# Prologue laid out anew: block 0 mixed half by VectorE and half by GpSimd, weight conversion and the third softmax moved into the first pairs

## Chip, core and metric

The kernel runs on one core of a Trainium2 chip. The metric is the device time of one execution in microseconds; before the change it is 2334.73 us (median of 3 runs, 2332.31 to 2334.87). The engines are named as in the profile: PE (TensorE, with its weight loads PEld), DVE (VectorE), ACT (ScalarE), POOL (GpSimd) and SP (SyncE, which issues the DMAs here).

## What is computed

The input `x` is (8, 4096, 192) in float32, `weight_gen` (8, 4096, 8, 7). A softmax over the seven taps of each token and head gives weights with which the token's row and the six rows before it are mixed, head by head (24 columns each). The result, 32768 rows of 192, goes through a feed-forward layer with 2048 hidden columns and a cosine:

```python
w = np.exp(weight_gen - max);  w = w / (sum(w) + 1e-9)      # over the 7 taps
x = einsum('bshk,bskhg->bshg', w, x_unfolded)               # causal, 7 rows
h = x @ w_in            # (32768, 192) @ (192, 2048)
g = h * np.cos(h)
return (g @ w_out).astype(np.float32)                       # (2048, 192)
```

`w_in` and `w_out` arrive as float64.

## The kernel before, in words

Each of the 128 partitions owns 256 consecutive rows. They are worked in 64 blocks of 4 rows (512 tokens of all partitions together). For each block the kernel mixes the rows (`attention`, L229), transposes the result on PE into x^T and splits it in a high part (fp32r) and a low part (`split`, L280). The hidden columns are worked in 8 pairs of 128-column chunks, so the main loop (L538) runs over 512 pairs, `i` = 0 to 511, and some turns more to drain.

One pair goes through these steps: PE computes h (`ffn_in_first` L313 and `ffn_in_second` L328, products of high and low parts); ACT writes the number of whole turns as an integer (`act_turns`, L349); DVE subtracts it from h (`dve_fraction`, L353); ACT takes the sine (`act_cos`, L357); DVE multiplies into g (`dve_g`, L360); ACT writes g's high part (`act_hi`, L367) and DVE its low part in bf16 (`dve_lo`, L371). Only then is the pair's PSUM tile free; there are three of these (`ps_h`). Six pairs later `ffn_out` (L377) multiplies g by `w_out`. `evacuate` (L409) lets ACT copy the sums out and POOL add them up.

All engines work through their instructions strictly in the order in which the program writes them, and the end of the kernel pins that order. In turn `i` of the loop the steps are written as: turns of pair i-1, high part of pair i-2, the third softmax's or a later one's Exp if it is due, the conversion of weights booked for this turn, fraction and sine of pair i-1, low part of pair i-2, g of pair i-1, then PE's work for pair i, the evacuation, the next weight load, one step of a softmax, and two to four steps of the background generator.

- **Mixing.** `attention(b, eng, ra, rb)` is written as 13 steps: a product for each of seven taps (L239) and six additions (L256), on the engine it is given. For blocks 1 to 63 this is POOL, step by step from the background generator `attentions` (L457), which also loads the rows two blocks ahead and waits for the softmax of its block.
- **Softmax.** `softmax` (L177) works on a batch of rows: a DMA of the taps, maximum (DVE, L190), subtraction (L192), Exp (ACT, L195), sum (L200), reciprocal (L206), product (L208). The first batch covers block 0, the second blocks 1 and 2, the third blocks 3 to 6; later ones four blocks each. Exp and the sine are different tables of ACT.
- **Weights.** `two_parts` (L105) turns float64 words into a float32 high part that PE can use and a low part: ACT takes the absolute value of the upper words (L116), DVE does four steps (L118, L121, L126, L130), ACT copies the high part (L132; for `w_out` also a bf16 copy, L134), POOL subtracts for the low part (L136). Its scratch tile `t1` shares four buffers with the `turn` tiles; `size` and `bits` are its two halves. The raw words land in buffers of the `ghi` tiles (`words`, L101). `w_in_a(c0, c1)` brings the first 128 rows of `w_in` for a range of columns in the layout that PE needs, `w_in_b(j)` a middle part of 512 columns, that is, for four pairs, and `w_out_2(q)` two chunks of `w_out`.
- **Booking.** The list `late` (L478) books conversions: an entry of period p is loaded two turns ahead and converted in turn p+1 (`converts`, popped with i-1).
- **Prologue** (L492 to L532). Loads: first taps, `w_in_b(0)`, `w_in_a(0, 256)`, block 0's rows, second taps, `w_in_a(256, 512)`, `w_in_b(1)`, block 1's rows, third taps, and two periods of `late`. Block 0 is mixed by POOL (row 3) and DVE (rows 0 to 2), the third softmax gets as far as its Exp, and ahead of the loop the chunks `a1` and `b1` are converted.
- **No-ops of SP.** `traded` (L266) has SP take part in the hand-over of a PSUM tile, so a no-op stands in SP's queue between the two halves of a pair, behind all DMAs issued before it.

Of the kernel before, what the change touches and what calls it, by code (L numbers as in the profile page):

```python
# [13 lines left out]
I32 = mybir.dt.int32  # L14
U16 = mybir.dt.uint16
BF16 = mybir.dt.bfloat16
AF = mybir.ActivationFunctionType
# [3 lines left out]
P = 128  # L21
# [20 lines left out]
def tile_softmax_conv_then_cos_ffn(  # L42
# [8 lines left out]
    nc = tc.nc  # L51

    B, S, D = x.shape
# [6 lines left out]
    R = 4  # L60
    NB = RPP // R
    CT = R * P
# [35 lines left out]
    wo = const.tile([P, NFC, 2 * D], F32R, name="wo")  # L98
    wo_b = const.tile([P, NFC, D], BF16, name="wo_b")

    def words(n):  # L101
        raw = gpool.tile([P, 2 * CW], I32, name="raw", tag="ghi")
        return raw[:, 0:2 * n]

    def two_parts(raw, hi, lo, half=None):  # L105
        shape = hi.shape[1:]
        n = math.prod(shape)

        def shaped(t, steps=1):
            t = t.rearrange("p (n s) -> p n s", s=steps)  # L110
            return t if len(shape) == 1 else t.rearrange("p (a b) s -> p a b s", b=shape[1])

        low, top = (shaped(raw, 2)[..., k] for k in range(2))
        t1 = work.tile([P, 2, CW], F32, name="t1", tag="turn", bufs=TMP)
        size, bits = (shaped(t1.bitcast(I32)[:, k, 0:n])[..., 0] for k in range(2))
        nc.scalar.activation(out=size.bitcast(F32), in_=top.bitcast(F32), func=AF.Abs)  # L116
        yield
        nc.vector.tensor_scalar(  # L118
            out=size.bitcast(F32), in0=size.bitcast(F32), scalar1=F64_SMALL, scalar2=None, op0=ALU.max)
        yield  # L120
        nc.vector.tensor_scalar(  # L121
            out=size, in0=size, scalar1=0x07FFFFFF, scalar2=3,
            op0=ALU.bitwise_and, op1=ALU.logical_shift_left)
        yield

        nc.vector.scalar_tensor_tensor(  # L126
            out=size, in0=top, scalar=-0x40000000, in1=size, op0=ALU.bitwise_and, op1=ALU.bitwise_or)
        yield

        nc.vector.scalar_tensor_tensor(  # L130
            out=bits, in0=low, scalar=29, in1=size, op0=ALU.logical_shift_right, op1=ALU.bitwise_or)
        nc.scalar.copy(out=hi, in_=bits.bitcast(F32))  # L132
        if half is not None:
            nc.scalar.copy(out=half, in_=bits.bitcast(F32))  # L134
        yield
        nc.gpsimd.tensor_tensor(out=lo, in0=bits.bitcast(F32), in1=hi.bitcast(F32), op=ALU.subtract)  # L136

    def w_in_a(c0, c1):
        raw = words(c1 - c0)
        for n in range(2):  # L140
            nc.sync.dma_start(out=raw[n * D2:(n + 1) * D2],
                              in_=w_in[n * P:n * P + D2, c0:c1].bitcast(I32))
        return two_parts(raw, wa_hi[:, c0:c1], wa_lo[:, c0:c1])
# [3 lines left out]
    def w_in_b(j):  # L147
        raw = words(CW)
        pairs = slice(j * CW // P, (j + 1) * CW // P)
        for n in range(2):  # L150
            nc.sync.dma_start(out=raw[n * D2:(n + 1) * D2].rearrange("k (a c) -> k a c", c=2 * P),
                              in_=w_in_odd_even[1 - n, D2:P, pairs, :].bitcast(I32))
        cols = slice(j * CW, (j + 1) * CW)
        return two_parts(raw, wb_hi[:, cols], wb_lo[:, cols])

    w_out_v = w_out.rearrange("(c p) d -> p c d", p=P)

    def w_out_2(q):
        raw = words(2 * D)
        nc.sync.dma_start(out=raw.rearrange("p (c d) -> p c d", c=2),  # L160
                          in_=w_out_v[:, 2 * q:2 * q + 2, :].bitcast(I32))
        cs = slice(2 * q, 2 * q + 2)
        return two_parts(raw, wo[:, cs, 0:D], wo[:, cs, D:2 * D], wo_b[:, cs, :])
# [51 lines left out]
    def load_rows(b):  # L215
        r0 = b * R
        xt = work.tile([P, R + PAD, D], F32, name="xt")
        rows[b] = xt
        first = max(0, PAD - r0)
        if first:  # L220
            nc.gpsimd.memset(xt[0:B, 0:first, :], 0.0)
            nc.sync.dma_start(
                out=xt[B:P, 0:first, :].rearrange("p r d -> p (r d)"),
                in_=x_v[0:P // B - 1, :, (RPP - first) * D:RPP * D])
        nc.sync.dma_start(
            out=xt[:, first:, :].rearrange("p r d -> p (r d)"),
            in_=x_v[:, :, (r0 - PAD + first) * D:(r0 + R) * D])
# [245 lines left out]
    def all_of(*steps):  # L473
        steps = list(steps)
        while steps:
            steps = [s for s in steps if next(s, steps) is not steps]

    late = [  # L478
        (0, w_in_a, (512, 1024)), (1, w_out_2, (0,)), (1, w_out_2, (1,)), (2, w_in_a, (1024, 1536)),
        (3, w_out_2, (2,)), (3, w_out_2, (3,)), (4, w_in_a, (1536, 2048)), (5, w_out_2, (4,)),  # L480
        (6, w_out_2, (5,)), (7, w_out_2, (6,)), (8, w_out_2, (7,)),
    ]
    SMP = 2
    AHEAD = 2
    converts = {}

    def load_weights(period):
        for at, load, args in late:
            if at == period:
                converts.setdefault(at, []).append(load(*args))  # L490

    nc.scalar.activation(out=early, in_=early, func=AF.Exp)  # L492
    sm0 = softmax(0, R, nc.vector)
    next(sm0)
    b0 = w_in_b(0)
    a0 = w_in_a(0, 256)
    load_rows(0)
    sm1 = softmax(R, 3 * R, nc.gpsimd)
    next(sm1)
    a1 = w_in_a(256, 512)  # L500
    b1 = w_in_b(1)
    load_rows(1)
    sm2 = softmax(3 * R, 3 * R + RW, nc.gpsimd)
    next(sm2)
    load_weights(0)
    load_weights(1)
    for _ in range(3):
        next(sm0)
    next(b0)
    next(a0)  # L510
    all_of(sm0)
    mix = attention(0, nc.gpsimd, 3, 4, spare=True)
    for _ in range(3):
        next(mix)
    all_of(b0, a0)
    next(mix)
    for _ in range(3):
        next(sm1)
    next(a1)
    next(b1)  # L520
    all_of(mix, attention(0, nc.vector, 0, 3))
    first = split(0, transpose_all(0), slice(0, CT), nc.vector)
    next(sm2)
    next(sm2)
    all_of(sm1)
    all_of(first)
    next(sm2)
    nc.scalar.activation(out=early, in_=early, func=AF.Sin)
    bg = attentions()
    for _ in range(4):  # L530
        next(bg)
    all_of(a1, b1)  # L532

    N = NB * NPAIR

    sm = sm2
    SOFTMAX = (0, 2, 3, 6, 7, 10, 11)
    for i in range(N + LAG + 1):  # L538
        b, pair = divmod(i, NPAIR)
        j = i - LAG  # L540
        step = i % (SB * NPAIR) - (SB - 1) * NPAIR
        if step < 0 and i >= SB * NPAIR:
            step += SB * NPAIR
        if step == 0 and b + 4 < NB:
            r0 = (b + 4) * R
            sm = softmax(r0, min(r0 + RW, RPP), nc.gpsimd, early=False)
        exps = step == SOFTMAX[3]

        whole = None
        if pair == TR and b + 1 <= WHOLE:  # L550
            until_mixed(b + 1)
            whole = transpose_all(b + 1)

        if 0 <= i - 1 < N:
            act_turns(i - 1)
        if 0 <= i - 2 < N:
            act_hi(i - 2)
        if exps:
            next(sm, None)
        now, later = list(splits), []  # L560
        splits.clear()
        if whole is not None:
            t = work.tile([P, 2, CT], F32, name="part0", bufs=3)
            nc.scalar.copy(out=t, in_=whole)
            later.append(split(b + 1, t, slice(0, CT), nc.vector))
        for c in converts.get(i - 1, ()):
            next(c)
        if 0 <= i - 1 < N:
            dve_fraction(i - 1)
            act_cos(i - 1)  # L570
        for c in now:
            next(c)
        splits.extend(later)
        all_of(*converts.pop(i - 1, ()))
        if 0 <= i - 2 < N:
            dve_lo(i - 2)
        if 0 <= i - 1 < N:
            dve_g(i - 1)
        all_of(*now)
        if i == N + LAG:  # L580
            break
        if b < NB and pair == 0:
            assert b in transposed
        if 0 <= j and j % (2 * R) == 0 and WHOLE < j // (2 * R) + 2 < NB:
            until_mixed(j // (2 * R) + 2)

        if whole is not None and j >= 0:
            ffn_out(j)
        if i < N:
            ffn_in_first(i, whole)  # L590
        if whole is None and j >= 0:
            ffn_out(j)
        if i < N:
            ffn_in_second(i)
        if j in stores:
            stores.pop(j)()
        if j >= 0:
            evacuate(j)
        load_weights(i + AHEAD)
        if step in SOFTMAX and not exps or NPAIR + SMP <= i < NPAIR + SMP + 3:  # L600
            next(sm, None)
        for _ in range(4 if i == 0 else 3 if i < 64 and i % 4 == 0 else 2):
            next(bg, None)
# [41 lines left out]
```

## Time and profile before

| | |
|---|---|
| runs before the change | 2334.73 us median, 2332.31 to 2334.87 |
| the profiled execution | 2332.66 us |
| its span in the profile | 2330.9 us |
| mean granted clock of PE | 0.982 |
| busy in the span: PE, PEld, DVE, ACT, POOL | 96%, 87%, 83%, 81%, 86% |
| pair 0, pair 1 and pair 12 start at | 32.1, 40.5 and 122.8 us |
| a pair in the steady part | 4.25 us |

A row of the timeline gives the start, the duration, the engine, the line of the kernel, the operation, out<-in by the program's names, the shapes and how many instructions the row holds; in brackets the time the engine stood idle before it and what ended that. A row of the stages gives a stretch, its length, the busy time (and number of instructions) of PE, PEld, DVE, ACT and POOL, the granted clock, the share of the DMA engines and GB/s. A row of a group gives busy time and mean nanoseconds.

### The profile page before, as it was taken

The numbers are of one execution on the slowest core, as the hardware profiler recorded it, in microseconds if no ns is written. First come the engines' busy times: TensorE is split into PE (matmuls) and PEld (weight loads), VectorE is DVE, ScalarE is ACT, GpSimd is POOL, SyncE is SP. The second block draws the span as 40 slices with busy tenths as digits, with TensorE's granted clock in tenths as the row PEclk, the third lists the DMA queues.
The fourth block names the chain that finished last, engine by engine and source line by source line (L and its number), as shares of the span: only waits on it lengthen the run. The fifth ranks groups of instructions, "written<-read, shape, count | busy, mean of one in ns | idle before, by whom it ended". The sixth has DMA issues, their size and how long they took to land.

```text
span 2330.9 us, 60541 instructions
## 1 busy us (share of the span) xinstructions
PE 2227.5 (96%) x26472; PEld 2033.6 (87%) x26472; DVE 1939.9 (83%) x1664; ACT 1898.8 (81%) x2123; POOL 2001.7 (86%) x1445
## 2 busy tenths in 40 slices
PE   2699999999999999999999999999999999999998
PEld 1488889999899888889998899899999999898897
DVE  8988887888888888888888888888888888888886
ACT  2677788888888888888888888888888888888885
POOL 6689889899898989989899889989889899889840
PEclk8799999999999999999999999999999999999999
DMA  6112112112212112112112212112112212212100
GB/s 145 45 42 57 35 47 49 40 42 49 50 32 57 35 39 57 42 40 49 42 40 49 50 32 57 42 32 57 43 40 49 52 30 49 50 32 51 32 8 22
DMA packets 25767, 105.55 MB, mean 45 GB/s; under 512 B 2734, under 2 KB 6566, under 8 KB 25502
## 3 DMA queue, kind: packets, MB, share of 16 engines
q1 hardware_dynamic: 25502, 101.67, 17.7%
q8 instruction: 208, 3.41, 0.6%
q14 instruction: 57, 0.47, 0.1%
HBM read 76.50 MB, written 25.17 MB: 44 GB/s over the span
## 4 chain that ended last, share of the span: by engine, by line
PE 65%; POOL 19%; DVE 7%; ACT 6%; issue 2%; DMA 0%; SPq 0%; POOLq 0%; ACTq 0%
PE acc L397 32%; PE h L339 21%; PE h L322 11%; POOL xa L256 6%; POOL pr L239 5%; POOL part L437 2%; DVE turn L353 2%; POOL x_lo L284 1%; DVE glo L371 1%; DVE h L360 1%; POOL fin L438 1%; ACT part L420 1%; ACT turn L349 1%; ACT turn L357 1%; POOL taps L192 1%
## 5 line engine op out<-in xcount | busy, mean ns | idle before, releaser
L353 DVE TENSOR_TENSOR turn<-h,turn 128x1024 f32<-128x1024 f32 x512 | 625.9, 1222 | 315.8 <-ACT turn L349 315.8
L397 PE MATMUL acc<-wo,ghi 64*128 64x384 f32 x8144 | 826.5, 339 | 3.0 <-ACT part L424 3.0
L397 PEld LDWEIGHTS acc<-wo,ghi 64*128 64x128 f32 x8144 | 753.8, 187 | 37.7 <-ACT part L424 3.9
L256 POOL TENSOR_TENSOR xa<-xa,pr 128x768 f32<-128x768 f32 (+1 forms) x384 | 709.0, 1846 | 0.6
L357 ACT ACTIVATE turn<-turn 128x1024 f32<-128x1024 f32 x512 | 543.4, 1061 | 196.3 <-DVE turn L353 196.1
L360 DVE SCALAR_TENSOR_TENSOR h<-h,turn 128x1024 f32<-128x1024 f32 x512 | 631.0, 1232 | 49.4 <-ACT turn L357 49.4
L349 ACT ACTIVATE turn<-h 128x1024 int32<-128x1024 f32 x512 | 525.7, 1027 | 159.9 <-PE h L339 158.2
L371 DVE TENSOR_TENSOR glo<-h,ghi 128x1024 bf16<-128x1024 f32 x512 | 621.9, 1215 | 1.1 <-ACT ghi L367 1.1
L239 POOL TENSOR_TENSOR pr<-xt,taps 128x768 f32<-128x768 f32 (+1 forms) x384 | 593.5, 1547 | 11.1
L367 ACT CAST ghi<-h 128x1024 fp32r<-128x1024 f32 x512 | 517.6, 1011 | 4.9 <-DVE h L360 3.6
L397 PE MATMUL acc<-wo_b,glo 64*128 64x192 bf16 x8144 | 434.0, 245 | 0.0
L437 POOL TENSOR_TENSOR part<-part,part 128x768 f32<-128x768 f32 x126 | 233.2, 1851 | 209.2 <-ACT part L420 164.5
L397 PEld LDWEIGHTS <-glo 64*128 64x128 bf16 x8144 | 340.3, 95 | 19.4 <-issue 4.8
L322 PE MATMUL h<-x_lo,wa_hi 64*128 64x512 f32 x1024 | 215.1, 404 | 61.9 <-DVE glo L371 48.5
L339 PE MATMUL h<-x_lo,wa_hi 64*128 64x512 f32 x1024 | 254.3, 481 | 1.0
L420 ACT COPY part<-acc 128x1024 f32<-128x1024 f32 x228 | 226.9, 995 | 0.0
L322 PE MATMUL h<-x_hi,wa_lo 64*128 64x512 f32 x1024 | 210.5, 394 | 1.3 <-POOL wa_lo L136 1.3
L339 PE MATMUL h<-x_lo,wb_hi 64*128 64x512 f32 x1024 | 211.7, 397 | 0.0
L339 PE MATMUL h<-x_hi,wa_hi 64*128 64x512 f32 x1024 | 211.4, 397 | 0.0
L322 PE MATMUL h<-x_hi,wa_hi 64*128 64x512 f32 x1024 | 211.0, 395 | 0.0
L339 PE MATMUL h<-x_hi,wa_lo 64*128 64x512 f32 x1024 | 208.7, 391 | 0.0
L339 PE MATMUL h<-x_hi,wb_lo 64*128 64x512 f32 x1024 | 208.6, 391 | 0.0
(68 smaller groups left out, 2162.1 us busy)
## 6 DMA issues: line engine op xcount, KB each, us to landing
xt<-in_x_dram SPq DMA_DIRECT2D x62, 960.0 KB, 6.8
out_dram<-fin SPq DMA_DIRECT2D x63, 384.0 KB, 3.4
taps<-in_weight_gen_dram SPq DMA_DIRECT2D x15, 448.0 KB, 4.8
raw<-in_moe_w_out_dram SPq DMA_DIRECT2D x8, 384.0 KB, 3.4
raw<-in_moe_w_in_dram SPq DMA_DIRECT2D x10, 256.0 KB, 4.3
xt<-in_x_dram SPq DMA_DIRECT2D x1, 768.0 KB, 10.5
xt<-in_x_dram SPq DMA_DIRECT2D x1, 540.0 KB, 6.6
raw<-in_moe_w_in_dram SPq DMA_DIRECT2D x4, 128.0 KB, 5.6
```

The costliest lines, as they stand in the source:

```text
L239: eng.tensor_tensor(out=dst.rearrange("p r (h g) -> p r h g", h=H), in0=xt[:, k + ra:k + rb, :].rearrange("p r (h g) -> p r h g", h=H), in ...
L256: eng.tensor_tensor(out=xa[:, ra:rb], in0=xa[:, ra:rb], in1=old[:, ra:rb], op=ALU.add)
L322: nc.tensor.matmul(h[:, q, :], lhsT=w[rs, chunk(pair, q)], rhs=v[rs, q, :], start=(m == 0), stop=False, skip_group_check=True)
L339: nc.tensor.matmul(h[:, 1 - q, :], lhsT=w[rs, cs], rhs=v[rs, q ^ middle, :], start=False, stop=(m == len(prods) - 1), skip_group_check=True)
L349: nc.scalar.activation(out=t.bitcast(I32), in_=hs[i], func=AF.Identity, bias=0.25, scale=1.0)
L353: nc.vector.tensor_tensor(out=t, in0=hs[i], in1=t.bitcast(I32), op=ALU.subtract)
L357: nc.scalar.activation(out=t, in_=t, func=AF.Sin, bias=SIN_BIAS, scale=SIN_SCALE)
L360: nc.vector.scalar_tensor_tensor(out=hs[i], in0=hs[i], scalar=TWO_PI, in1=turns.pop(i), op0=ALU.mult, op1=ALU.mult)
L367: nc.scalar.copy(out=hi, in_=hs[i])
L371: nc.vector.tensor_tensor(out=lo, in0=hs.pop(i), in1=hi.bitcast(F32), op=ALU.subtract)
L397: nc.tensor.matmul(to, lhsT=g[rs, n, t * P:(t + 1) * P], rhs=w[rs, fc, :], start=(lo == 0 and c == 0 and (whole or s == 0)), stop=(lo == 1 ...
L437: eng.tensor_tensor(out=part, in0=part, in1=old, op=ALU.add)
```

## The change

Block 0 is mixed half by DVE (rows 0 and 1) and half by POOL (rows 2 and 3), and its rows are loaded directly behind the first taps. The second softmax's subtraction and last product go from POOL to DVE. Of the weights only `b0` and `a0` are converted ahead of the loop; columns 256 to 512 become period 0, `w_in_b(1)` period 3, and the others are booked anew. The third softmax runs entirely in the loop, in turns 3 to 8 (`EARLY`), where its last three steps stood in turns 10 to 12. All loads of periods 0 to 7 are issued ahead of the loop; four of them and the last two land in buffers of `fin` and `part1`. The scratch tile of the conversion holds `size` and `bits` in alternate words where it held them in two halves.

```diff
-    def words(n):
-        raw = gpool.tile([P, 2 * CW], I32, name="raw", tag="ghi")
+    def words(n, home="ghi"):
+
+        if home == "ghi":
+            raw = gpool.tile([P, 2 * CW], I32, name="raw", tag=home)
+        elif home == "fin":
+            raw = work.tile([P, R * D], I32, name="raw", tag=home)
+        else:
+            raw = work.tile([P, 2 * CT], I32, name="raw", tag=home)
         return raw[:, 0:2 * n]
...
-        size, bits = (shaped(t1.bitcast(I32)[:, k, 0:n])[..., 0] for k in range(2))
+        t1 = t1.bitcast(I32).rearrange("p a b -> p (a b)")[:, 0:2 * n]
+        size, bits = (shaped(t1, 2)[..., k] for k in range(2))
...
     late = [
-        (0, w_in_a, (512, 1024)), (1, w_out_2, (0,)), (1, w_out_2, (1,)), (2, w_in_a, (1024, 1536)),
-        (3, w_out_2, (2,)), (3, w_out_2, (3,)), (4, w_in_a, (1536, 2048)), (5, w_out_2, (4,)),
-        (6, w_out_2, (5,)), (7, w_out_2, (6,)), (8, w_out_2, (7,)),
+        (0, w_in_a, (256, 512)), (1, w_in_a, (512, 1024)), (2, w_out_2, (0,)), (3, w_in_b, (1,)),
+        (3, w_in_a, (1024, 1536)), (4, w_out_2, (1,)), (4, w_out_2, (2,)),
+        (5, w_in_a, (1536, 2048, "part1")), (5, w_out_2, (3, "part1")), (6, w_out_2, (4, "fin")),
+        (7, w_out_2, (5, "fin")), (8, w_out_2, (6, "part1")), (9, w_out_2, (7, "part1")),
     ]
...
     sm0 = softmax(0, R, nc.vector)
     next(sm0)
+    load_rows(0)
     b0 = w_in_b(0)
     a0 = w_in_a(0, 256)
-    load_rows(0)
-    sm1 = softmax(R, 3 * R, nc.gpsimd)
+    sm1 = softmax(R, 3 * R, nc.vector)
     next(sm1)
-    a1 = w_in_a(256, 512)
-    b1 = w_in_b(1)
     load_rows(1)
+    for period in range(3):
+        load_weights(period)
     sm2 = softmax(3 * R, 3 * R + RW, nc.gpsimd)
     next(sm2)
...
+    for period in range(3, 8):
+        load_weights(period)
...
     all_of(sm0)
-    mix = attention(0, nc.gpsimd, 3, 4, spare=True)
-    for _ in range(3):
-        next(mix)
+    mix_v = attention(0, nc.vector, 0, 2)
+    mix_p = attention(0, nc.gpsimd, 2, 4, spare=True)
+    go_on(mix_v, 3)
+    go_on(mix_p, 5)
+    go_on(b0, 1)
+    go_on(a0, 1)
+    go_on(mix_v, 2)
     all_of(b0, a0)
...
+    go_on(sm1, 3)
+    go_on(mix_v, 3)
+    go_on(mix_p, 3)
+    go_on(sm1, 1)
+    go_on(mix_v, 2)
+    all_of(sm1)
+    nc.scalar.activation(out=early, in_=early, func=AF.Sin)
+    all_of(mix_v)
+    all_of(mix_p)
     first = split(0, transpose_all(0), slice(0, CT), nc.vector)
-    next(sm2)
-    next(sm2)
-    all_of(sm1)
     all_of(first)
-    next(sm2)
-    nc.scalar.activation(out=early, in_=early, func=AF.Sin)
     bg = attentions()
...
-    all_of(a1, b1)
...
+    EARLY = (3, 4, 5, 6, 7, 8)
...
-        exps = step == SOFTMAX[3]
+        exps = step == SOFTMAX[3] or i == EARLY[2]
...
-        load_weights(i + AHEAD)
-        if step in SOFTMAX and not exps or NPAIR + SMP <= i < NPAIR + SMP + 3:
+        if i + AHEAD >= 8:
+            load_weights(i + AHEAD)
+        if (step in SOFTMAX or i in EARLY) and not exps:
             next(sm, None)
```

More of the change, by code (lines that the diff above doesn't have):

```diff
@@ L107, in two_parts, with shaped @@
         n = math.prod(shape)
-        def shaped(t, steps=1):
+        def shaped(t, steps):
             t = t.rearrange("p (n s) -> p n s", s=steps)
@@ L136, in two_parts, with w_in_a @@
         nc.gpsimd.tensor_tensor(out=lo, in0=bits.bitcast(F32), in1=hi.bitcast(F32), op=ALU.subtract)
-    def w_in_a(c0, c1):
-        raw = words(c1 - c0)
+    def w_in_a(c0, c1, home="ghi"):
+        raw = words(c1 - c0, home)
         for n in range(2):
@@ L156, in tile_softmax_conv_then_cos_ffn, with w_out_2 @@
     w_out_v = w_out.rearrange("(c p) d -> p c d", p=P)
-    def w_out_2(q):
-        raw = words(2 * D)
+    def w_out_2(q, home="ghi"):
+        raw = words(2 * D, home)
         nc.sync.dma_start(out=raw.rearrange("p (c d) -> p c d", c=2),
@@ L478, in tile_softmax_conv_then_cos_ffn @@
     late = [
-        (0, w_in_a, (512, 1024)), (1, w_out_2, (0,)), (1, w_out_2, (1,)), (2, w_in_a, (1024, 1536)),
-        (3, w_out_2, (2,)), (3, w_out_2, (3,)), (4, w_in_a, (1536, 2048)), (5, w_out_2, (4,)),
-        (6, w_out_2, (5,)), (7, w_out_2, (6,)), (8, w_out_2, (7,)),
+        (0, w_in_a, (256, 512)), (1, w_in_a, (512, 1024)), (2, w_out_2, (0,)), (3, w_in_b, (1,)),
+        (3, w_in_a, (1024, 1536)), (4, w_out_2, (1,)), (4, w_out_2, (2,)),
+        (5, w_in_a, (1536, 2048, "part1")), (5, w_out_2, (3, "part1")), (6, w_out_2, (4, "fin")),
+        (7, w_out_2, (5, "fin")), (8, w_out_2, (6, "part1")), (9, w_out_2, (7, "part1")),
     ]
-    SMP = 2
     AHEAD = 2
@@ L494, in tile_softmax_conv_then_cos_ffn, with go_on @@
     next(sm0)
+    load_rows(0)
     b0 = w_in_b(0)
     a0 = w_in_a(0, 256)
-    load_rows(0)
-    sm1 = softmax(R, 3 * R, nc.gpsimd)
+    sm1 = softmax(R, 3 * R, nc.vector)
     next(sm1)
-    a1 = w_in_a(256, 512)
-    b1 = w_in_b(1)
     load_rows(1)
+    for period in range(3):
+        load_weights(period)
     sm2 = softmax(3 * R, 3 * R + RW, nc.gpsimd)
     next(sm2)
-    load_weights(0)
-    load_weights(1)
-    for _ in range(3):
-        next(sm0)
-    next(b0)
-    next(a0)
-    all_of(sm0)
-    mix = attention(0, nc.gpsimd, 3, 4, spare=True)
-    for _ in range(3):
-        next(mix)
-    all_of(b0, a0)
[L516 to L521, printed above, removed]
+    for period in range(3, 8):
+        load_weights(period)
+    def go_on(steps, n):
+        for _ in range(n):
+            next(steps, None)
+    all_of(sm0)
+    mix_v = attention(0, nc.vector, 0, 2)
[5 more added lines that the diff above has]
+    go_on(mix_v, 2)
+    all_of(b0, a0)
+    go_on(sm1, 3)
[7 more added lines that the diff above has]
+    all_of(mix_p)
     first = split(0, transpose_all(0), slice(0, CT), nc.vector)
-    next(sm2)
-    next(sm2)
-    all_of(sm1)
     all_of(first)
-    next(sm2)
-    nc.scalar.activation(out=early, in_=early, func=AF.Sin)
     bg = attentions()
-    for _ in range(4):
-        next(bg)
-    all_of(a1, b1)
+    go_on(bg, 4)
     N = NB * NPAIR
     sm = sm2
+    EARLY = (3, 4, 5, 6, 7, 8)
     SOFTMAX = (0, 2, 3, 6, 7, 10, 11)
```

## The prediction

> **What bounds it.** I read the page first, then busy time by stage, then by pair, and last the prologue instruction by instruction.
>
> ```profile
> span 2330.9 us, 60541 instructions
> ...
> PE 65%; POOL 19%; DVE 7%; ACT 6%; issue 2%; DMA 0%; SPq 0%; POOLq 0%; ACTq 0%
> ```
> ```profile
> 31.90:118.50 86.60, 54.36 (x366) 38.18 (x368) 79.69 (x84) 47.57 (x67) 59.44 (x40) 0.76 0.24 63
> ...
> 217.00:2331.00 2114.00, 2077.58 (x25024) 1912.40 (x25024) 1755.06 (x1481) 1765.86 (x1963) 1834.43 (x1326) 0.99 0.17 43
> ```
> The second fence gives a stretch, its length, then the busy time of PE, PEld, DVE, ACT and POOL, the granted clock, the DMA share and GB/s. From 217 us on TensorE is busy 2077.6 of 2114 us, and nothing that the change touches shortens its work. From 31.9 to 118.5 us it is busy 54.4 of 86.6 us and DVE 79.7: there DVE sets the pace. The chain gives POOL 19%, but POOL is no bound in the long part; this is the waits between 432 and 572 us:
>
> ```profile
> POOL part L437 <- ACT part L420: 11.2, 8, 3.1
> ```
> POOL waits there for ACT. So the change is worth what it moves the moment from which pairs follow at the steady pace, the start of pair 12. In the next fence each stretch runs from one pair's first matmul to the next one's, for pairs 0 to 6, and the last from pair 6 to pair 12; below it the row of pair 2.
>
> ```profile
> 32.10:40.53 8.43, 4.57 (x18) 2.63 (x18) 8.43 (x8) 1.29 (x3) 7.00 (x4) 1.00 0.64 146
> 40.53:51.25 10.72, 4.71 (x18) 2.50 (x18) 8.94 (x7) 3.82 (x6) 9.28 (x6) 0.51 0.34 100
> 51.25:59.86 8.61, 4.94 (x19) 2.64 (x19) 8.01 (x12) 5.34 (x10) 5.80 (x5) 0.50 0.24 61
> 59.86:67.46 7.60, 4.58 (x18) 2.72 (x19) 7.05 (x8) 4.74 (x7) 4.67 (x4) 0.68 0.17 52
> 67.46:77.49 10.03, 5.79 (x27) 3.55 (x28) 8.74 (x13) 7.80 (x13) 6.65 (x6) 0.70 0.13 42
> 77.49:83.02 5.53, 4.46 (x18) 2.67 (x19) 4.89 (x6) 2.70 (x4) 3.06 (x3) 0.61 0.20 71
> 83.02:122.76 39.74, 29.56 (x300) 25.29 (x302) 36.91 (x38) 25.30 (x34) 22.80 (x15) 0.91 0.14 35
> ```
> ```profile
> 51.25 0.79 PE L322 MATMUL h<-x_lo,wa_hi 64*128 64x512 f32 x2 [5.67 <-ACT wa_hi L132]
> ```
> A pair's own eighteen matmuls take 4.6 to 4.9 us here, its interval 5.5 to 10.7. Pair 2 waited 5.7 us for a converted weight (the step that ACT's copy into wa_hi ends).
>
> **The prologue.** Today DVE mixes three rows of block 0 (576 elements) and POOL one (192). The rows of both engines in order of start, and DVE's last additions:
>
> ```profile
> 18.46 1.03 DVE L239 TENSOR_TENSOR pr<-xt,taps 128x576 f32<-128x576 f32 x1
> 18.95 0.92 POOL L239 TENSOR_TENSOR pr<-xt,taps 128x192 f32<-128x192 f32 x1
> 19.41 1.07 DVE L256 TENSOR_TENSOR xa<-xa,pr 128x576 f32<-128x576 f32 x1
> 19.83 1.10 POOL L256 TENSOR_TENSOR xa<-xa,pr 128x192 f32<-128x192 f32 x1
> ```
> ```profile
> 25.58 1.93 DVE L256 TENSOR_TENSOR xa<-xa,pr 128x576 f32<-128x576 f32 x2
> ```
> ```profile
> 163.53 1.85 POOL L256 TENSOR_TENSOR xa<-xa,pr 128x768 f32<-128x768 f32 x1
> 165.46 1.54 POOL L239 TENSOR_TENSOR pr<-xt,taps 128x768 f32<-128x768 f32 x1
> ```
> The ends alternate: DVE 19.49, POOL 19.87, DVE 20.48, POOL 20.93. The steps between them, 0.38, 0.61 and 0.45, are what each instruction needs alone: the two engines take turns instead of running beside each other. Half each gives both 384 elements: DVE 0.41 (0.61 x 384/576); POOL, read between its 192 and 768 rows, 0.75 for a product (0.38, 1.54) and 0.92 for an addition (0.45, 1.85). A product and its addition on both engines then cost 0.41+0.75+0.41+0.92 = 2.49 us in turns, against 0.61+0.38+0.61+0.45 = 2.05 today, because more goes to the slower engine. The Trainium skill speaks against this part of the change (SBUF — State Buffer, "Who interferes with whom"): a DVE instruction with two SBUF inputs and a GpSimd one that reads SBUF exclude each other for a whole instruction. By that rule the sum below holds; without it, the third rival's does.
>
> ```profile
> 5.62 0.39 DVE L208 TENSOR_TENSOR taps<-taps,den 128x224 f32<-128x224 f32 x1
> 7.26 0.43 DVE L118 TENSOR_SCALAR t<-t 128x512 f32<-128x512 f32 x1 [1.25 <-ACT t L116]
> ...
> 9.83 1.02 DVE L130 SCALAR_TENSOR_TENSOR t<-raw,t 128x512 int32<-128x512 int32 x2
> ```
> ```profile
> GB/s 81 236 234 216 219 226 189 0 49 228 109 190 0 38 93 80 18 103 4 0 98 4 252 92 0 0 0 0 4 0 0 4 0 0 179 71 94 8 0 0
> ```
> ```profile
> 50.58 0.62 ACT L132 CAST wa_hi<-t 128x512 fp32r<-128x512 f32 x1 [5.94 <-DVE t L130]
> 51.11 1.02 ACT L349 ACTIVATE turn<-h 128x1024 int32<-128x1024 f32 x1
> ```
> ```profile
> 51.28 1.27 POOL L136 TENSOR_TENSOR wa_lo<-t,wa_hi 128x512 fp32r<-128x512 f32 x1 [1.28 <-ACT wa_hi L132]
> ```
> The rows of x are now loaded ahead of b0 and a0. At some 225 GB/s (the figures of the GB/s row are for 4 us each) their first transfer of 0.55 MB lands near 6.3, behind the taps, which are ready at 6.0 as today. From there, in the new order: five mixing steps on each engine in turns, 5x0.41 + 4x0.75 + 0.92 = 6.0, to 12.3. Then DVE converts b0 and a0 alone, while POOL stands, since its next instructions are their low parts: 3.6 us today (7.26 to 10.85) with a gap of 0.5 in it, so 3.1, to 15.4. ACT's copy 0.5, the low parts 1.3 and 0.7 and the second softmax's subtraction, now DVE's, 0.5: 18.4. The eight steps left on each: 8x0.41 + 3x0.75 + 5x0.92 = 10.1, and 0.6 for that softmax's other turns: 29.1. POOL is through first and gets block 1's first product (1.5) in before DVE's last addition: 30.6, where today mixing ends at 27.5. From there to pair 0 it is 4.6 us today, 4.4 without the reciprocal that stands in front of x_lo. Pair 0 starts near 35.0 in place of 32.1: **2.9 later**. The DMAs moved ahead of the loop cost nothing: 28 transfers of 8.2 MB land by about 38, with eight in flight the last is issued near 28, and SyncE's first no-op, which pair 0's second half waits for, is due at 36. Should that margin of 8 us go, pair 0 waits by the rest. Their buffers (ghi, fin, part1) have no earlier user.
>
> **The first pairs.** Today columns 256-512 are converted ahead of the loop, and each later 512 columns of w_in one pair before their use. After the change each is converted in the turn of the pair that needs it (pairs 1, 2, 4 and 6), and on DVE behind the fraction of the pair before. That closes a circle with no overlap in it: matmuls of pair i-1, ACT's turns, DVE's fraction, four DVE steps, ACT's copy, POOL's low part, pair i.
>
> ```profile
> 60.84 1.23 DVE L353 TENSOR_TENSOR turn<-h,turn 128x1024 f32<-128x1024 f32 x1
> 62.51 1.75 DVE L118 TENSOR_SCALAR t<-t 128x512 f32<-128x512 f32 x1 [0.45 <-ACT t L116]
> 64.30 0.43 DVE L121 TENSOR_SCALAR t<-t 128x512 int32<-128x512 int32 x1
> 64.76 0.69 DVE L126 SCALAR_TENSOR_TENSOR t<-raw,t 128x512 int32<-128x512 int32 x1
> ```
> What the circle gives back: the first of these conversion steps took 1.75 us while POOL was mixing, the next 0.43 when POOL stood. In the circle POOL has mostly run out of the work issued to it, so four steps of 512 cost 2x0.43 + 2x0.69 = 2.2, of 384 some 1.8, of 256 1.4. The new scratch layout (size and bits in alternate words) is in no row. The two short steps may cost 0.43 as now or 0.69 like the steps that read `raw` at that stride; I take 0.43, from the same instruction at the same length. The other end is 0.5 for each of thirteen conversions, some 3 us on the path, and as much may come off if those two steps then no longer take turns with POOL.
>
> The new intervals, today's in brackets. 0-1: matmuls 4.7, turns 1.0, fraction 1.2, steps 1.4, copy 0.4, handovers 0.3: 9.0 (8.4). 1-2: 4.8+1.0+1.2+2.2+0.6 and handovers: 10.0 (10.7). 2-3: matmuls and half a us for a low part: 5.2 (8.6); this pair gains, since DVE is through in time. 3-4: 4.7, ACT still at the copies of w_out 0.5, turns 1.0, DVE still at the third softmax's maximum 1.1, fraction 1.2, two conversions of 512 3.8, copies 0.6: 12.9 (7.6). 4-5: two low parts 1.4, matmuls 4.7, turns and hi 1.9, then the moved Exp and the copy of the transposed block 1.0: 11.2 (10.0). This Exp is priced by a later softmax's:
>
> ```profile
> 492.20 1.28 ACT L195 ACT_TABLE_LOAD   x1
> 493.49 0.96 ACT L195 ACTIVATE taps<-taps 128x896 f32<-128x896 f32 x1
> 494.46 1.28 ACT L357 ACT_TABLE_LOAD   x1
> ```
> Ahead of the loop it needed no table load of its own; inside it brings two, 3.5 us of ACT, of which 2.2 lie before the copy that pair 5 waits for, and the rest beside its matmuls. 5-6: 4.8+1.0+1.2, ACT's hi and absolute value first 0.5, steps for w_in and w_out 3.5, one POOL product in front 1.5, copy 0.5: 12.9 (5.5). 6-12: pair 6 with a low part and ffn_out 5.8; pairs 7 and 8 5.3 and 6.5 (DVE's three steps 3.6, w_out 1.8, the softmax's sum or reciprocal 1.0); pair 9 10.3, as three of w_out's steps meet POOL mixing block 2 (1.9 each); pair 10 9.5, since the last w_out is now converted in the turn whose ffn_out needs it; pair 11 4.2: 41.6 (39.7). The sum is 102.8 against 90.7: **12.1 later**. That the third softmax is ready sooner lets POOL start on block 3 sooner, which is worth nothing where POOL ends up waiting for ACT.
>
> Together 15.0 us. The profiled execution took 2332.66 us, span 2330.9 and 1.8 around it, so 2347.7; the median of the runs lies 2.1 above it, hence **2350**. The landing times, the scratch layout and who comes first at some five meetings of DVE and POOL (up to 1.9 each) give this case a range of its own of 2343 to 2355.
>
> **Rivals.** Faster: pairs 1, 2, 4 and 6 do not wait for their weights, because DVE converts them beside the matmuls of the pair before. Their intervals (9.0, 10.0, 12.9, 12.9) fall to 5.2 each, 24.0 less, and the sum to 9 us below today's: 2326. For it speaks that POOL no longer stretches the steps, against it that the code puts them behind the fraction of that same pair. No change: half of this circle is hidden, 12 us less: 2338, within 0.2%. Halves side by side: POOL alone needs 7x0.75 + 6x0.92 = 10.8 from 6.3 on, and 5.1 for waiting and low parts; mixing ends at 22.2, 8.4 earlier: 2341.5. The alternating ends speak against it. Slower still, the clock:
>
> ```profile
> 90.77 1.60 PE L397 MATMUL acc<-wo,ghi 64*128 64x384 f32 x16
> ...
> 98.49 2.51 PE L397 MATMUL acc<-wo,ghi 64*128 64x384 f32 x16
> ```
> Sixteen equal matmuls take 2.51 in place of 1.60 us in a pair that came after a wait. Counting the rest of such a pair, 1.7 us more in each of pairs 6, 10 and 11, where the circle leaves gaps, make 2355. The Trainium skill has the rule (TensorE: Matmul & The Clock Gate, Part 1): an idle window of about 3.4 us halves the clock; the granted clock of 0.50 to 0.70 in the first pairs agrees.
>
> **Numbers.** Forecast 0.55, clock 0.13, side by side 0.11, faster 0.12, no change 0.09. Slower by over 0.2% (4.7 us, about what a measurement of this kernel can tell from no change) gathers 0.79. The range of 2338 to 2357 holds these three cases; the faster one stays outside.
>
> **What would show it.** Pair 0 near 35; mixing still alternating, its end near 30.6; pairs 1, 2, 4 and 6 released by wa_hi or wa_lo, DVE idle for ACT's turns before them; two table loads ahead of pair 5; pair 12 near 138; and 4.2 us a pair from there. I am wrong if pair 12 starts before 127 us, or if a later stretch gains or loses.

## The result, and the profile after

The changed kernel takes 2353.53 us (median of 4 runs, 2351.98 to 2354.7) against 2333.86 us before (4 runs on the same chip): a ratio of 1.0084, interval 1.0067 to 1.0102. It is 19.7 us slower. Its profiled execution took 2354.7 us, its span is 2352.9 us, the mean granted clock 0.977.

The head of its page and its chain's shares by engine:

```profile
span 2352.9 us, 60542 instructions
...
PE 67%; POOL 17%; DVE 7%; ACT 6%; issue 3%; DMA 0%; SPq 0%; POOLq 0%; ACTq 0%; DVEq 0%
```

The chain has the same shape as before, give or take two per cent; it hides the change. The stages show it. Below are the pairs 0 to 5, each from its first matmul to the next pair's, then pair 6 to pair 12, and the long rest (columns as in the prediction: stretch, length, busy PE, PEld, DVE, ACT, POOL, granted clock, DMA share, GB/s):

```profile
33.69:44.10 10.41, 4.57 (x18) 2.64 (x18) 4.50 (x6) 2.83 (x4) 8.35 (x5) 0.88 0.59 159
44.10:54.69 10.59, 4.68 (x20) 2.61 (x20) 4.86 (x7) 4.09 (x5) 4.03 (x3) 0.66 0.00 0
54.69:60.10 5.41, 4.74 (x18) 2.93 (x20) 1.53 (x2) 0.00 (x0) 4.58 (x3) 0.50 0.00 0
60.10:73.64 13.54, 3.33 (x21) 1.91 (x18) 11.96 (x18) 9.71 (x13) 3.34 (x3) 0.63 0.00 1
73.64:84.82 11.18, 5.68 (x26) 3.46 (x26) 2.75 (x3) 5.11 (x6) 8.20 (x6) 0.65 0.01 3
84.82:97.56 12.74, 4.58 (x19) 2.64 (x20) 11.70 (x20) 10.57 (x16) 5.46 (x4) 0.63 0.00 0
97.56:142.07 44.51, 31.80 (x301) 26.59 (x302) 34.55 (x37) 22.96 (x32) 25.75 (x17) 0.86 0.17 40
...
217.00:2353.00 2136.00, 2096.46 (x25218) 1923.09 (x25214) 1769.11 (x1492) 1782.21 (x1979) 1847.15 (x1334) 0.99 0.18 42
```

Pair 12 starts at 142.07 where it was 122.76: 19.3 us of the loss are there by then, 1.6 of them before pair 0. From pair 0 to pair 12 DVE was busy 83.0 of 90.7 us before and is now busy 71.9 of 108.4; TensorE was busy 58.7 and is now busy 59.4: nobody is full, everybody waits in turn. The first matmuls of the pairs tell for whom (TensorE's timeline, the release in brackets):

```profile
44.10 0.79 PE L329 MATMUL h<-x_lo,wa_hi 64*128 64x512 f32 x2 [5.75 <-ACT wa_hi L139]
54.69 0.80 PE L329 MATMUL h<-x_lo,wa_hi 64*128 64x512 f32 x2 [5.78 <-ACT wa_hi L139]
60.10 0.62 PE L329 MATMUL h<-x_lo,wa_hi 64*128 64x512 f32 x2
73.64 0.79 PE L329 MATMUL h<-x_lo,wa_hi 64*128 64x512 f32 x2 [10.11 <-ACT wa_hi L139]
84.82 0.79 PE L329 MATMUL h<-x_lo,wa_hi 64*128 64x512 f32 x2 [4.16 <-ACT part L575]
97.56 0.79 PE L329 MATMUL h<-x_lo,wa_hi 64*128 64x512 f32 x2 [8.07 <-ACT wa_hi L139]
```

Pairs 1, 2, 4 and 6, the four whose columns of `w_in` are converted in their own turn, wait for exactly that copy. Pair 3, which needs nothing new, waits for nothing. DVE's timeline in pair 3 shows the order that closes the circle: third softmax's maximum, fraction of pair 3, then eight steps for two weights that pair 4 stands still for (x2 rows hold a step of each weight):

```profile
66.94 1.08 DVE L197 TENSOR_REDUCE top<-taps 128x128 f32<-128x896 f32 x1
67.93 1.21 DVE L360 TENSOR_TENSOR turn<-h,turn 128x1024 f32<-128x1024 f32 x1
69.06 0.76 DVE L125 TENSOR_SCALAR t<-t 128x512 f32<-128x512 f32 x2
69.72 0.76 DVE L128 TENSOR_SCALAR t<-t 128x512 int32<-128x512 int32 x2
70.40 1.29 DVE L133 SCALAR_TENSOR_TENSOR t<-raw,t 128x512 int32<-128x512 int32 x2
71.60 1.29 DVE L137 SCALAR_TENSOR_TENSOR t<-raw,t 128x512 int32<-128x512 int32 x2
```

### The profile page after: what moved, and what is told of

The parts are those of the page before. It is cut to its first block, busy times and chain, and to the rows that moved or that the text cites. A ratio compares the mean times of both kernels' runs of the same rounds, so it can differ in the third digit from the quotient of the medians.

```text
span 2352.9 us, 60542 instructions
## 1 busy us (share of the span) xinstructions
PE 2230.3 (95%) x26472; PEld 2031.0 (86%) x26472; DVE 1930.1 (82%) x1666; ACT 1902.4 (81%) x2125; POOL 2002.6 (85%) x1443
## 4 chain that ended last, share of the span: by engine, by line
PE 67%; POOL 17%; DVE 7%; ACT 6%; issue 3%; DMA 0%; SPq 0%; POOLq 0%; ACTq 0%; DVEq 0%
PE acc L404 33%; PE h L346 22%; PE h L329 11%; POOL xa L263 6%; POOL pr L246 5%; DVE turn L360 2%; POOL part L444 2%; POOL x_lo L291 1%; ACT turn L356 1%; DVE glo L378 1%; ACT part L427 1%; DVE h L367 1%; POOL fin L445 1%; ACT turn L364 1%; POOL taps L199 1%
## 6 DMA issues: line engine op xcount, KB each, us to landing
xt<-in_x_dram SPq DMA_DIRECT2D x1, 768.0 KB, 10.2
```

## The experiments

The theory is the prediction's: weights converted in the turn that needs them cost most of it, and mixing by halves, in turns with POOL, a little. Rivals: the moved Exp with its two table loads, the scratch layout, POOL's meetings with DVE. The runs of the kernel before on the same chips had medians of 2332.7 to 2332.9 us; ratios are to those. The positions below (pair 12 and so on) are of the profiled executions.

**The booking undone.** The changed kernel with the weights booked a turn earlier:

```diff
-        (0, w_in_a, (256, 512)), (1, w_in_a, (512, 1024)), (2, w_out_2, (0,)), (3, w_in_b, (1,)),
-        (3, w_in_a, (1024, 1536)), (4, w_out_2, (1,)), (4, w_out_2, (2,)),
-        (5, w_in_a, (1536, 2048, "part1")), (5, w_out_2, (3, "part1")), (6, w_out_2, (4, "fin")),
-        (7, w_out_2, (5, "fin")), (8, w_out_2, (6, "part1")), (9, w_out_2, (7, "part1")),
+        (0, w_in_a, (256, 512)), (0, w_in_a, (512, 1024)), (1, w_out_2, (0,)), (2, w_in_b, (1,)),
+        (2, w_in_a, (1024, 1536)), (3, w_out_2, (1,)), (4, w_out_2, (2,)),
+        (4, w_in_a, (1536, 2048, "part1")), (5, w_out_2, (3, "part1")), (6, w_out_2, (4, "fin")),
+        (7, w_out_2, (5, "fin")), (8, w_out_2, (6, "part1")), (8, w_out_2, (7, "part1")),
```

> The changed kernel with one thing altered: the weights of pairs 2, 4 and 6 and the last w_out chunk are converted one turn ahead of their use, as before the change; the mixing in halves, the moved Exp and the new scratch layout stay. Theory (the circle of just-in-time conversion costs the time): pair 2, 4 and 6 follow their predecessors after some 5, 9 and 6 us where it was 10.6, 13.5 and 12.7, some of it coming back in other turns; pair 12 starts near 129 us in place of 142.1 and the time is near 2340, 13 us under the changed kernel. Rival (the prologue, the Exp or the layout costs it): pair 12 stays at 139 or later and the time within 3 us of 2353.5.

Measured: 2338.35 us (10 runs), ratio 1.0025 (1.0016 to 1.0034); pair 12 at 128.2. Its pairs 1 to 4 on TensorE's timeline, and four late matmuls of `ffn_out` in pair 6:

```profile
45.09 0.80 PE L329 MATMUL h<-x_lo,wa_hi 64*128 64x512 f32 x2 [6.65 <-ACT wa_hi L139]
49.93 0.40 PE L329 MATMUL h<-x_lo,wa_hi 64*128 64x512 f32 x2
55.81 0.50 PE L329 MATMUL h<-x_lo,wa_hi 64*128 64x512 f32 x2 [3.26 <-DVE glo L378]
64.48 0.80 PE L329 MATMUL h<-x_lo,wa_hi 64*128 64x512 f32 x2 [4.70 <-DVE glo L378]
...
89.64 1.01 PE L404 MATMUL acc<-wo,ghi 64*128 64x384 f32 x4 [4.05 <-POOL wo L143]
```

Pair 2 follows with no wait, and pair 4 waits 4.7 us, for DVE's low part of a pair, where it waited 10.1 us for a weight. The kernel is 5.5 us slower than the kernel before on the same chip, where the changed kernel is 19.7 slower: the booking is worth some 14 us. What is left is not the start alone. Pair 1 starts at 45.1 where it was 40.5 before, for it still gets its columns in its own turn, now with a second conversion beside them; but pair 6 starts at 82.0, 1.0 us ahead of the kernel before (83.0). The loss comes back in pairs 6 to 11, which take 46.2 us in place of 39.7. Pair 6 alone takes 12.3 where it took 7.0: its `ffn_out` waits 4.05 us (last line) for `w_out_2(3)`, two chunks of `w_out` that this booking still converts in the turn that needs it. So the rest is in good part the same circle once more; that is read from the trace, and no run isolates it.

**The booking alone.** The kernel before, only `w_in` booked just in time:

```diff
-        (0, w_in_a, (512, 1024)), (1, w_out_2, (0,)), (1, w_out_2, (1,)), (2, w_in_a, (1024, 1536)),
-        (3, w_out_2, (2,)), (3, w_out_2, (3,)), (4, w_in_a, (1536, 2048)), (5, w_out_2, (4,)),
+        (0, w_out_2, (0,)), (1, w_in_a, (512, 1024)), (2, w_out_2, (1,)), (3, w_in_a, (1024, 1536)),
+        (4, w_out_2, (2,)), (4, w_out_2, (3,)), (5, w_in_a, (1536, 2048)), (5, w_out_2, (4,)),
```

> The kernel before, in which only the booking of w_in is changed: columns 512 to 1024, 1024 to 1536 and 1536 to 2048 are converted in the turn of the pair that needs them (pairs 2, 4 and 6) where the kernel before converts them one pair ahead; the first pieces of w_out move up. If a conversion without a pair of lead is what costs the changed kernel its time, the pairs 2, 4 and 6 now close the same circle: interval 1-2 from 10.7 to about 17, 3-4 from 7.6 to about 11, 5-6 from 5.5 to about 12.8, while 2-3 and 4-5 give back some 3 us each; pair 12 near 130 where it is 122.8, and about 2341 us. Rival: the booking is innocent and the time went with the other parts of the change; then pair 12 stays within 2 us of 122.8 and the time within 2 us of the kernel before.

Measured: 2345.93 us (4 runs), ratio 1.0059 (1.0044 to 1.0074); pair 12 at 134.5. The rival falls. Pairs 2, 4 and 6 on TensorE's timeline:

```profile
58.42 0.80 PE L322 MATMUL h<-x_lo,wa_hi 64*128 64x512 f32 x2 [12.42 <-ACT wa_hi L132]
...
75.51 0.80 PE L322 MATMUL h<-x_lo,wa_hi 64*128 64x512 f32 x2 [8.07 <-ACT wa_hi L132]
...
96.77 0.79 PE L322 MATMUL h<-x_lo,wa_hi 64*128 64x512 f32 x2 [9.87 <-ACT wa_hi L132]
```

The three intervals came as expected (17.4, 11.7, 12.6). Pair 12 moved by 11.7, not by 7 to 8, and the time by 13 in place of 8; but the expectation's total did not follow from its own intervals, which are 17.0 us longer less some 6 given back, that is, 11. Given back were 3.2 in 2-3, 1.4 in 4-5 and 2.0 in pairs 6 to 11. From both sides the booking is worth 13 to 14 us.

**The third softmax ahead of the loop again.** The changed kernel with `go_on(sm2, 3)` in front of the table load for the sine and `EARLY = (6, 7, 8)`:

> The changed kernel with the third softmax's maximum, subtraction and Exp put ahead of the loop again, in front of the change to the sine table; its last three steps stay in turns 6 to 8. Theory (the Exp is a side cost): pair 5 follows pair 4 after 9.0 us in place of 11.2, but DVE's maximum (1.1) and POOL's subtraction (1.75) make the prologue 1 to 2 us longer, so pair 12 moves by less than 2 us either way and the time stays within 3 us of 2353.5. Rival (the two table loads are what the change costs): 3.5 us or more come off pair 12 and the time.

Measured: 2356.23 us, ratio 1.0097 (1.008 to 1.0114). Interval 4-5 fell from 11.2 to 9.2, as the price of 2.2 for the table loads said; but pair 0 started 3.5 us later, at 37.2, where I expected 1 to 2, and pair 12 at 144.1. The moved Exp did not cost the change its time.

**Three rows and one.** The changed kernel, block 0 split as before (`attention(0, nc.vector, 0, 3)`, `attention(0, nc.gpsimd, 3, 4, spare=True)`):

> The changed kernel with block 0 mixed as before the change, three rows by DVE and one by POOL. Theory (the engines take turns, so POOL's larger share only lengthens the sum): a product with its addition on both engines takes 2.05 us in place of about 2.45, mixing ends 2 to 3 us sooner, near 27, pair 0 starts near 31; the gain is partly lost behind POOL's block 1, the time falls by 1 to 3 us. Rival (the halves run side by side and the change's split is right): mixing ends later than the 29.3 us of the changed kernel, because DVE has more to do.

Measured: 2352.32 us, ratio 1.0084 (1.0069 to 1.0099). Mixing ends at 28.8 in place of 29.2, less than I expected: POOL, through with its one row at 25.3, gets block 1's first product (25.30 to 27.35) in before DVE's last addition. Interval 0-1 falls to 9.0; pair 12 at 141.2. The split is worth about 1 us here, which the time cannot tell from nothing.

**The old scratch layout.** The changed kernel, `size` and `bits` in two halves again:

> The changed kernel with the scratch tile of the conversion laid out in halves as before. Theory (the layout is worth nothing, since the two short DVE steps take 0.43 us for 512 words in both): pair starts within 1 us of the changed kernel's, the time within 2 us. Rival (alternate words slow or speed the conversion by 0.26 us a short step): pair 12 moves by 3 us or more.

Measured: 2352.93 us, ratio 1.0088 (1.0073 to 1.0103). No effect that the time can tell. Pairs 0 to 6 start within 0.3 us of the changed kernel's; pair 12 starts at 143.5, 1.4 later, which is more than I expected but less than the rival's 3. A step of 384 elements takes 0.36 us in either layout.

**The split alone.** The kernel before, POOL mixing rows 2 and 3:

```diff
-    mix = attention(0, nc.gpsimd, 3, 4, spare=True)
+    mix = attention(0, nc.gpsimd, 2, 4, spare=True)
...
-    all_of(mix, attention(0, nc.vector, 0, 3))
+    all_of(mix, attention(0, nc.vector, 0, 2))
```

> The kernel before, in which only the split of block 0 is changed: DVE mixes rows 0 and 1, POOL rows 2 and 3 (before: DVE three rows, POOL one). Nothing else of the prologue moves. If the engines take turns, a product and its addition cost 2.49 us on both in place of 2.05, 6.5 times, so pair 0 starts 2.9 us later, at 35.0 in place of 32.1; should DVE slip its last addition in ahead of POOL's first product of block 1, as in the changed kernel, about 1.5 less. Pair 12 moves by as much. Rival, side by side: POOL's half alone needs 10.8 us and DVE's less, mixing ends 2 us or more earlier and pair 0 starts at 30 or before.

Measured: 2334.38 us, ratio 1.0006 (0.9997 to 1.0015). Pair 0 starts at 34.4, 2.3 later, between the two ends, and pair 12 at 126.3, 3.5 later; the time cannot be told from no change. DVE's last rows:

```profile
24.82 1.34 DVE L256 TENSOR_TENSOR xa<-xa,pr 128x384 f32<-128x384 f32 x1
26.20 1.10 DVE L239 TENSOR_TENSOR pr<-xt,taps 128x384 f32<-128x384 f32 x1
27.22 2.61 DVE L256 TENSOR_TENSOR xa<-xa,pr 128x384 f32<-128x384 f32 x2
```

A third fewer elements than in the kernel before, and each instruction stands longer (1.34 against 1.07). An addition follows the one before after 2.40 us (24.82, 27.22), where it was 2.06 in the kernel before (19.41, 21.47) and the prediction's sum gives 2.49: the halves do not run side by side.

**POOL's half left out.**

```diff
-    mix_p = attention(0, nc.gpsimd, 2, 4, spare=True)
+    mix_p = iter(())
+    nc.gpsimd.memset(mixed[0][:, 2:4, :], 0.0)
```

> The changed kernel without GpSimd's half of block 0: rows 2 and 3 of that block are zeros in place of the mixed rows. If the two engines take turns, a DVE step of 384 elements, which comes every 1.2 to 1.3 us in the changed kernel, comes every 0.45 to 0.5 us, and mixing ends 5 us or more ahead of 29.2 us. Rival, side by side: DVE keeps its pace and its end.

Measured: 2349.64 us, a single execution. DVE's end of block 0, first in the changed kernel, then here:

```profile
22.56 0.55 DVE L246 TENSOR_TENSOR pr<-xt,taps 128x384 f32<-128x384 f32 x1
23.02 1.21 DVE L263 TENSOR_TENSOR xa<-xa,pr 128x384 f32<-128x384 f32 x1
...
25.49 1.21 DVE L246 TENSOR_TENSOR pr<-xt,taps 128x384 f32<-128x384 f32 x1
26.63 2.61 DVE L263 TENSOR_TENSOR xa<-xa,pr 128x384 f32<-128x384 f32 x2
```
```profile
20.38 0.55 DVE L246 TENSOR_TENSOR pr<-xt,taps 128x384 f32<-128x384 f32 x1
20.85 0.55 DVE L263 TENSOR_TENSOR xa<-xa,pr 128x384 f32<-128x384 f32 x1
...
22.44 0.55 DVE L246 TENSOR_TENSOR pr<-xt,taps 128x384 f32<-128x384 f32 x1
22.91 2.49 DVE L263 TENSOR_TENSOR xa<-xa,pr 128x384 f32<-128x384 f32 x2
```

The same step is 0.55 us alone and 1.21 beside POOL: turns are shown. (The product at 22.56 is not stretched in the changed kernel either; there it was POOL's product, from 22.54 on, that stood 1.28 us, where the prediction estimates 0.75 for it alone.) Mixing ends at 25.4, 3.8 earlier and not 5, because here POOL did slip block 1's first product in (22.66 to 24.40) ahead of DVE's last addition: two additions that alone take 0.55 each fill 2.49 us.

**Block 1 on DVE, in the changed kernel:** `attention(b, nc.vector if b == 1 else nc.gpsimd)`.

> The changed kernel with block 1 mixed by DVE in place of POOL. If POOL, still mixing block 1, is what made interval 0-1 10.4 us where the circle needs 9.0, that interval falls to about 9 and pair 0 does not start later; the other intervals keep their lengths, since the circle is closed by DVE and ACT; pair 12 near 140 (142.1) and about 2351 us. Rival: the meetings with POOL stretch all of the first pairs and the bookings only seem to; then pairs 2, 4 and 6 gain too and pair 12 starts before 135.

Measured: 2352.6 us, ratio 1.0088 (1.0074 to 1.0102). The rival falls: pairs 2, 4 and 6 gain nothing, pair 12 starts at 143.4. For interval 0-1 (10.2) the run decides nothing, since DVE's own mixing step now stands in front of the fraction (40.80 in place of 39.50); but the suspected step itself shrank. Fraction and first conversion step, in the changed kernel, then here:

```profile
39.50 1.23 DVE L360 TENSOR_TENSOR turn<-h,turn 128x1024 f32<-128x1024 f32 x1 [5.87 <-ACT turn L356]
40.64 1.71 DVE L125 TENSOR_SCALAR t<-t 128x256 f32<-128x256 f32 x1
```
```profile
40.80 1.22 DVE L360 TENSOR_TENSOR turn<-h,turn 128x1024 f32<-128x1024 f32 x1
41.93 0.29 DVE L125 TENSOR_SCALAR t<-t 128x256 f32<-128x256 f32 x1
```

**What helps.** Three versions of the kernel before, its booking kept. First block 1 on DVE alone (the edit just shown):

> The kernel before with block 1 mixed by DVE in place of POOL, in the background of pairs 0 to 7 as before. A step of 768 elements costs DVE about 0.8 us where it costs POOL 1.5 to 1.85, and while POOL works a step DVE's own conversion step takes 1.75 us in place of 0.43. If POOL's mixing beside the conversions is what stretches the first pairs, pair 12 starts near 116 (122.8 before) and the time is 2326 to 2329. Rival: DVE, which is busy 92% of the first pairs, is the bound and has 13 more steps to do, some 10 us; then pair 12 comes 3 us or more later than before and the time is 2336 or more.

Measured: 2329.95 us, ratio 0.9984 (0.9975 to 0.9994); pair 12 at 119.8, 3.0 earlier where I expected 6.8. A part of that is that DVE's step of 768 elements takes 0.95 us and not 0.8, some 2 us over thirteen steps; the rest is open. Then blocks 0, 1 and 2 on DVE (`b <= 2`, and `all_of(attention(0, nc.vector, 0, 4))`):

> The kernel before with block 0 mixed by DVE alone (POOL has no part in it) and blocks 1 and 2 by DVE too. If the engines take turns and POOL is the slower one, block 0 in DVE's hands alone costs 13 steps of 0.8 = 10.4 us in place of 7x1.0 + 6x1.05 = 13.3: mixing ends some 2 us earlier and pair 0 starts at 29 to 30.5 (32.1 before); with blocks 1 and 2 on DVE pair 12 starts at 111 to 114 and the time is 2322 to 2325. Rival, side by side: DVE's steps of block 0 grow with the rows, from 1.0 to 1.37, mixing ends 4 us later, and pair 12 starts no earlier than 122.

Measured: 2328.86 us, the same ratio and interval; pair 0 at 31.5, pair 12 at 119.7 and not at 111 to 114. Blocks 0 and 2 on DVE together add nothing that can be told: DVE is busy 85.9 of the 88.2 us from pair 0 to pair 12. Last, the one idle stretch of DVE that the change does remove, its wait for block 0's rows:

```diff
     next(sm0)
+    load_rows(0)
     b0 = w_in_b(0)
     a0 = w_in_a(0, 256)
-    load_rows(0)
...
     all_of(sm0)
-    all_of(b0, a0)
+    all_of(attention(0, nc.vector, 0, 4))
     for _ in range(3):
         next(sm1)
+    first = split(0, transpose_all(0), slice(0, CT), nc.vector)
+    next(first)
+    all_of(b0, a0)
     next(a1)
     next(b1)
-    all_of(attention(0, nc.vector, 0, 4))
-    first = split(0, transpose_all(0), slice(0, CT), nc.vector)
+    all_of(first)
     next(sm2)
     next(sm2)
     all_of(sm1)
-    all_of(first)
```

(against the version with three blocks on DVE; block 2 is POOL's again).

> The kernel before with the one piece of the change that removes idle time of DVE: block 0's rows are loaded directly behind the first taps. DVE mixes all of block 0 from 7.2 us on, then converts b0 and a0 while TensorE transposes and ACT copies; block 1 is mixed by DVE, the booking stays as before. 13 steps of 0.93 us end near 19.5 us (27.5 before), pair 0 starts at 25 to 26 (32.1). The steps of the second and third softmax that stood ahead of x_lo, 3.4 us of DVE, move behind it, and DVE is the bound of the first pairs, so of the 6 to 7 us some 3 remain against the run with block 1 on DVE: pair 12 at 116 to 117 (119.8 there, 122.8 before), 2326 to 2327 us. Rival: SyncE's no-op behind the loads, or the words of the weights, hold pair 0's second half, and pair 12 starts at 119 or later.

Measured: 2327.18 us (9 runs), ratio 0.9976 (0.9967 to 0.9986): 5.6 us below the kernel before and the lowest median here, though its interval overlaps those of the two versions above. DVE's first and last mixing steps:

```profile
7.22 0.96 DVE L239 TENSOR_TENSOR xa<-xt,taps 128x768 f32<-128x768 f32 x1 [1.17 <-DMA xt<-in_x_dram]
...
17.28 1.94 DVE L256 TENSOR_TENSOR xa<-xa,pr 128x768 f32<-128x768 f32 x2
```

Mixing ends at 19.2, pair 0 starts at 24.8 and pair 12 at 117.4. Of the 7.3 us won at pair 0, 5.4 remain at pair 12; 3.0 of these are there with block 1 on DVE alone.

## Why the prediction held, step by step

The forecast was 2350, the measurement 2353.5. Direction and cause were right; the terms of the sum differ. The prologue was given 1.3 us too much and the first pairs 5.6 too little, so it is luck that the total is nearer than the larger of its terms.

- **Prologue, +2.9 foretold, +1.6 measured.** Turns were right (0.55 us alone, 1.21 beside POOL). The Trainium skill's rule (SBUF — State Buffer, "Who interferes with whom") agrees with that. The term that failed is "POOL is through first and gets block 1's first product (1.5) in before DVE's last addition". In the changed kernel DVE's addition came first: mixing ends at 29.24 (26.63 + 2.61), 1.4 before the 30.6 I gave it. Without POOL's half, and with three rows and one, it went the other way. A smaller error cancelled: the rows came at 7.2 and not near 6.3, yet the second half of the mixing began at 18.2, where I had 18.4.
- **First pairs, 102.8 foretold, 108.4 measured.** The circle is there, and the releases are those foretold. Interval by interval, foretold and measured: 9.0 and 10.4, 10.0 and 10.6, 5.2 and 5.4, 12.9 and 13.5, 11.2 and 11.2, 12.9 and 12.7, 41.6 and 44.5.
- **Interval 0-1, 1.4 short.** I wrote that POOL "has mostly run out of the work issued to it". In pair 0 it had not: it started block 1 at 28.8, and its addition of 40.39 to 42.20 stretched DVE's first conversion step, which alone takes 0.29, to 1.71 us. With the three-and-one split that step takes 0.28, and the interval is the foretold 9.0.
- **Scratch layout.** The value taken, 0.43 us for 512 elements, holds; the run with the old layout agrees.
- **Moved Exp.** Two table loads ahead of pair 5, interval 11.2 as foretold.
- **Pairs 6 to 12, 2.9 short.** This is a piece of the clock rival, in pairs 6 and 10 (sixteen equal matmuls in pairs 6 and 7, then pair 10's last four, which wait for the last piece of `w_out`; the granted clock is 0.61 in pair 6, 1.00 in pair 7 and 0.68 in pair 10):

```profile
99.95 2.76 PE L404 MATMUL acc<-wo,ghi 64*128 64x384 f32 x16
...
105.58 1.59 PE L404 MATMUL acc<-wo,ghi 64*128 64x384 f32 x16
...
133.74 0.99 PE L404 MATMUL acc<-wo,ghi 64*128 64x384 f32 x4 [3.02 <-POOL wo L143]
```

Pairs 6 and 10 take 7.3 and 10.5 where I had 5.8 and 9.5; pairs 7 to 9 and 11 together are 0.4 off. The clock's part was only read from these rows; no run isolates it.

- **"A later stretch gains or loses".** After pair 12 the changed kernel's profiled execution takes 2.7 us more than that of the kernel before, against what I wrote. 1.5 of it is in the tail from pair 504 on (57.9 us in place of 56.4), nearly all at one group, first of the changed kernel, then of the kernel before:

```profile
2335.38 2.93 PE L404 MATMUL acc<-wo,ghi 128*128 128x384 f32 x8 [2.08 <-ACT part L431]
```
```profile
2314.90 1.67 PE L397 MATMUL acc<-wo,ghi 128*128 128x384 f32 x8 [2.07 <-ACT part L424]
```

The same work after the same wait runs slower; the granted clock in it is 0.50, and 1.00 in the kernel before. The Trainium skill has the clock's window run freely, not reset when a kernel starts (TensorE: Matmul & The Clock Gate, Part 1). That would explain why the same wait costs time in one execution and not in another; it does not explain why 2.1 us are enough, less than the 3.4 that it names as a window. Over all profiled executions the tail takes 56.3 to 56.4 or 57.9 to 58.0 us. The longer value stands in four of the seven of the changed kernel and its variants, and in none of the six of the kernel before and its variants. The stretch from pair 12 to pair 64 takes 239.3 to 240.2 us in the seven and 238.2 to 239.2 in the six. So some 1 to 2 us behind pair 12 may belong to the change; no run decides it.

- **The rivals.** Conversions hidden, half hidden, and halves side by side are shown wrong. Two parts of the change were not run alone: the loads moved ahead of the loop and the second softmax's steps on DVE. The loads did not hold pair 0, whose second half follows its first without a wait in TensorE's timeline (35.43 us), and the version with the booking undone keeps both parts and is some 14 us faster. What I left out was the front of the prologue as an opportunity: the idle time there was DVE's wait for rows, and half each spends it on turns.

## What to carry over

Before moving work closer to its use, follow the releases round once: if producer and user wait for each other through one in-order queue, nothing is hidden, however idle the engines look afterwards; a pair of lead was worth 13 to 14 us here. Splitting a step over two engines pays only if each engine's steps stay as short as they are alone. Rows that overlap in the trace don't show that, since a row also holds the engine's wait for its turn; ends that alternate say that the engines take turns. In a stage where one engine is full, look for its idle stretches ahead of the stage and fill those first: that gave the lowest median here, if by little over block 1 on DVE alone.

## What the hardware showed unexpectedly

- Beside POOL, cutting DVE's share by a third buys nothing: an addition of 384 elements takes 1.21 us beside POOL's steps of 384, one of 576 takes 1.07 beside POOL's steps of 192, and 0.55 is what 384 take alone.
- Whether DVE's last addition or POOL's next product goes first moves the end of mixing by some 1.4 us (without POOL's half DVE's two additions stand 2.49 us, where two of 0.55 take 1.10), and it differs between versions of the kernel that differ only in the split.
